# Two weight transfers in attention instead of three, early gathers split around a weight transfer, and smaller sink tiles

## The chip, the core and the metric

The kernel runs on one core of one Trainium2 chip. The metric is device microseconds for one execution. The time before is the median of 14 runs, 231.12 us. One further execution was taken with the hardware profiler, and all rows below are from it.

## The reference

Two layers follow one another. First, attention with 4 batches, 8 heads, 768 positions and head size 64. Three heads (0, 2 and 6) are causal over everything; the other five see the first 4 positions (the "sink") and a window of 64. Then a mixture of 8 experts over the 3072 tokens: a token's expert is given by `domain_id`, and no gate is computed.

```python
scores = scale * np.matmul(q, k.transpose(0, 1, 3, 2))
stream_keep = causal & (is_sink | in_win)       # heads that are not retrieval heads
a = softmax(np.where(mask, scores, -1e9))
x = np.matmul(a, v).transpose(0, 2, 1, 3).reshape(B * S, H * D)
for e in range(E):                              # 8 experts, D = 512, F = 1024
    mask = domain_id == e
    out[mask] = np.maximum(x[mask] @ w1[e], 0.0) @ w2[e]
```

## The kernel before

**Attention** is a loop over n = 0 to 16. Each n below 16 is a pair of heads of one batch: b = n // 4, and the pair is one of (0,2), (6,7), (1,3), (4,5). Iteration n computes the scores of pair n on PE (L302) and their exponentials on ACT (L339), transposes q and k of pair n+1 (PE L282, copied out by DVE L288), and multiplies the probabilities of pair n-1 with v (PE L391, "av", one PSUM tile for each of the two heads). DVE then divides by the row sums: a reciprocal (L403) and a multiply into the batch's tile `xb` (L404). Two PSUM buffers serve the transposes and the av tiles in turn, so an av tile waits for the multiply of the tile two before it. The last iteration, n = 16, has only the av of pair 15.

Ahead of each iteration `hooks(n)` queues the side work. SP loads q, k and v of pair n+4. POOL casts q and k of pair n+2 to 16 bits (L156), then v of pair n+1 (`cast_v`, L176, L180). `cast_v` also copies the 4 sink rows of v into the small tiles `vs`, which the av of streaming heads reads. When n is 5, 9 or 13, SP stores the finished batch `xb` to `x_tok` in DRAM (L415); the last batch is stored after the loop. POOL's queue also takes weight transfers (`load_w`, L187 for the first layer, L193 for the second; each reads 32-bit weights and writes 1 MB of 16-bit weights) and gathers (`load_xe`, L658), which fetch 128 tokens of an expert pair from `x_tok` by an index list. Every engine takes its own instructions in the order in which they stand.

**Routing** puts every token into a slot of its expert and makes the index lists on DVE, one item for each step of the loop; the last item is done in iteration 9.

**Experts** come in pairs pr = 0 to 3. A pair has seven gathers, g = 0 to 6. For pairs 0 and 1, g = 0, 1, 3 and 4 are the *early* gathers: they need only the tokens of batches 0 to 2 and are put into `hooks(14)`. Their tiles `xe` are cleared first by DVE (in `hooks(13)`). The early tokens go through the first layer (`layer1(e, 0, EARLY)`, PE L703, ACT L710) while the last batch is stored; then POOL gathers g = 2, 5 and 6, which need that store. Each gather is transposed on PE (`x_transpose`, L675) and copied out by DVE (L688, L682). The second layer (PE L754, L768) is copied out by DVE (L717) and scattered to `out` by POOL (L719).

The schedule is written by hand. What stands around the change:

```python
ws = {4: (0, 1), 8: (1, 1), 12: (2, 1)}
if n in ws:
    load_w(*ws[n])
...
if n == 14:
    for pr in range(2):
        for g in (0, 1, 3, 4):
            load_xe(pr, g, 3)
    load_w(3, 1)
```

After the loop the order is: `store_x(3)`; `x_transpose` of the early gathers of pair 0; `load_xe(0, 2/5/6)`; `load_w(0, 2)`; `load_xe(1, 2/5/6)`; `load_w(1, 2)`; four gathers of pair 2; `layer1` of expert 0's early tokens; `x_transpose` of pair 1's early gathers; `layer1` of experts 1, 2 and 3; then the transposes of g = 2, 5 and 6.

Of the kernel before, what the change touches and what calls it, by code (L numbers as in the profile page):

```python
# [9 lines left out]
FP16 = mybir.dt.float16  # L10
# [7 lines left out]
P = 128  # L18
# [3 lines left out]
def kernel(  # L22
# [14 lines left out]
    B, H, S, D = q.shape  # L37
    NTOK, DM = out.shape
    E, _, F = moe_w1.shape
    NS = int(n_sink)  # L40
# [13 lines left out]
    NSLOT = E * CAP  # L54
    PAIRS = [(0, 2), (6, 7), (1, 3), (4, 5)]
    NPAIR = B * len(PAIRS)
    scale = float(1.0 / np.sqrt(D))


# [49 lines left out]
    cpool = ctx.enter_context(tc.tile_pool(name="consts", bufs=1))  # L109
# [19 lines left out]
    out_i = cpool.tile([P, NSLOT // P], I32, name="out_i")  # L129
    flag_i = cpool.tile([1, 1], I32, name="flag_i")  # L130
    vs_t = [
        [cpool.tile([P, H, D + 1], FP16, name=f"vs{i}_{x}") for x in range(2)] for i in range(2)
    ]


    q32_t, qk_t, v_t, ve_t, w_t = {}, {}, {}, {}, {}
# [4 lines left out]
    def load_qk(n):  # L141
        b, pi = divmod(n, 4)
        hA, hB = PAIRS[pi]
        for nm, src in (("q", q), ("k", k)):
            t = qkpool.tile([P, 2, NSO, D], FP32, tag=nm, name=f"{nm}32_{n}")
            nc.sync.dma_start(
                out=t[:].rearrange("p h t d -> p h (t d)"),
                in_=hsel(src, b, hA, hB).rearrange("h (p t) d -> p h (t d)", p=P),
            )
            q32_t[nm, n] = t  # L150
# [19 lines left out]
    def cast_v(b, pi):  # L170
        if pi == 0:
            ve_t[b] = vepool.tile([P, NSO, H, D + 1], FP16, tag="ve", name=f"ve_{b}")
            nc.gpsimd.memset(ve_t[b][:, :, :, D : D + 1], 1.0)
        hA, hB = PAIRS[pi]
        for hh, h in enumerate((hA, hB)):
            nc.gpsimd.tensor_copy(out=ve_t[b][:, :, h, 0:D], in_=v_t[b, pi][:, hh])  # L176
        for hh, h in enumerate((hA, hB)):
            if not retr[h]:
                x = 1 if hh and not retr[hA] else 0
                nc.gpsimd.tensor_copy(  # L180
                    out=vs_t[b % 2][x][64 * x : 64 * x + NS, h, :], in_=ve_t[b][0:NS, 0, h, :]
                )

    def load_w(e, which):
        if which == 1:
            t = wpool.tile([P, 2, 2, F], FP16, tag="w1", name=f"w1_{e}")
            nc.gpsimd.dma_start(  # L187
                out=t[:].rearrange("p c r f -> p c (r f)"),
                in_=moe_w1[e].rearrange("(c p r) f -> p c (r f)", p=P, r=2),
            )  # L190
        else:
            t = wpool.tile([P, 2, 4, DM], FP16, tag="w2", name=f"w2_{e}")
            nc.gpsimd.dma_start(  # L193
                out=t[:].rearrange("p c r d -> p c (r d)"),
                in_=moe_w2[e].rearrange("(c p r) d -> p c (r d)", p=P, r=4),
            )
        w_t[e, which] = t
# [64 lines left out]
    def col_of(tiles, hh, jt, i):  # L262
        for n, (chunks, c0, c1) in enumerate(tiles):
            for c, h2, j2, i0, w in chunks:
                if (h2 == hh or (h2 == 2 and jt == "s")) and j2 == jt and i0 <= i < i0 + w:
                    return n, c + i - i0
        raise KeyError((hh, jt, i))
# [91 lines left out]
    def av_items(n):  # L359
        b, pi = divmod(n, 4)  # L360
        tiles = plans[pi]
        items = []
        for hh, h in enumerate(PAIRS[pi]):
            both_s = not any(retr[x] for x in PAIRS[pi])
            mms = []
            if retr[h]:
                for it in range(NSO):
                    for jt in range(it + 1):
                        mms.append((it, jt, 0, P))
            else:  # L370
                for it in range(NSO):
                    mms.append((it, it, 0, P))
                for it in range(2, NSO):
                    mms.append((it, "s", 0, P))
                mms.append((1, "s", 64, P))
                for it in range(1, NSO):
                    mms.append((it, it - 1, 0, 64))
            cell = {}

            def mm(x, h=h, hh=hh, mms=mms, cell=cell, both_s=both_s):  # L380
                it, jt, m0, m1 = mms[x]
                if x == 0:
                    cell["ps"] = ps_b.tile([P, 512], FP32, tag="b", name=f"av_{n}_{hh}")
                ps = cell["ps"][:, 0 : NSO * (D + 1)].rearrange("p (t d) -> p t d", t=NSO)
                r, c = col_of(tiles, hh, jt, it * P + m0)
                w = m1 - m0
                if jt == "s":
                    rhs = vs_t[b % 2][int(both_s and hh == 1)][:, h, :]
                else:
                    rhs = ve_t[b][:, jt, h, :]  # L390
                nc.tensor.matmul(  # L391
                    out=ps[m0:m1, it, :],
                    lhsT=eT[n, r // 3][:, r % 3, c : c + w],
                    rhs=rhs,
                    start=(x == 0),
                    stop=(x == len(mms) - 1),
                    skip_group_check=True,
                )
                if x == len(mms) - 1:
                    if b not in xb:  # L400
                        xb[b] = xpool.tile([P, NSO, DM], FP16, tag="xb", name=f"xb_{b}")
                    rcp = tpool.tile([P, NSO], FP32, tag="rcp", name=f"rcp_{n}_{hh}")
                    nc.vector.reciprocal(out=rcp[:], in_=ps[:, :, D])  # L403
                    nc.vector.tensor_tensor(  # L404
                        out=xb[b][:, :, h * D : (h + 1) * D],
                        in0=ps[:, :, 0:D],
                        in1=rcp[:].unsqueeze(2).to_broadcast([P, NSO, D]),
                        op=ALU.mult,
                    )

            items.append([lambda x=x, mm=mm: mm(x) for x in range(len(mms))])
        return items

# [233 lines left out]
    def xe_of(pr, g):  # L647
        u, o = (2 * pr + g // 3, g % 3) if g < 6 else ((pr, "h"), 0)
        if u not in xe_t:
            if g < 6:  # L650
                xe_t[u] = qkpool.tile([P, 3, DM], FP16, tag="qk"[u % 2], name=f"xe_{u}")
            else:
                xe_t[u] = vpool.tile([P, 1, DM], FP16, tag="v32", name=f"xeh_{pr}")
        return xe_t[u][:, o, :]

    def load_xe(pr, g, nb=B):
        s = pr * NG + g
        nc.gpsimd.indirect_dma_start(  # L658
            out=xe_of(pr, g),
            out_offset=None,  # L660
            in_=x_d[0 : 1 + nb * S, :],
            in_offset=bass.IndirectOffsetOnAxis(ap=map_i[:, s : s + 1], axis=0),
            bounds_check=nb * S,
            oob_is_err=False,
        )
# [135 lines left out]
    def hooks(n):  # L801
        b, pi = divmod(n, 4)
        if n + 4 < NPAIR:
            load_qk(n + 4)
            load_v((n + 4) // 4, (n + 4) % 4)
        if n + 2 < NPAIR:
            cast_qk(n + 2)
        if n + 1 < NPAIR:
            cast_v((n + 1) // 4, (n + 1) % 4)
        if n >= 5 and n % 4 == 1:  # L810
            store_x(n // 4 - 1)
        ws = {4: (0, 1), 8: (1, 1), 12: (2, 1)}
        if n in ws:
            load_w(*ws[n])
        if n == 13:
            for u in range(4):
                xe_of(u // 2, 3 * (u % 2))
                nc.vector.memset(xe_t[u][:, 0:2, :], 0.0)
        if n == 14:
            for pr in range(2):  # L820
                for g in (0, 1, 3, 4):
                    load_xe(pr, g, 3)
            load_w(3, 1)

    def run(fns):
# [5 lines left out]
    route = routing_items()  # L831
    for n in range(NPAIR + 1):
        if n < NPAIR:
            hooks(n)
        T = t_items(n + 1) if n + 1 < NPAIR else {"q": [], "k": []}
        A, B_ = av_items(n - 1) if n >= 1 else ([], [])
# [5 lines left out]
        else:  # L842
            h = len(B_) // 2
# [56 lines left out]
    with tc.If(nc.values_load(flag_i[0:1, 0:1], min_val=0, max_val=2) > 0, preferred_fallthrough_block=False):  # L900
        x_v = x_d[1 : 1 + NTOK, :].rearrange("(b p s) d -> b s p d", b=B, p=P)
        with tc.For_i(0, B, 1) as gb, tc.For_i(0, NSO, 1) as gs:
# [3 lines left out]
                out=g_d64[:], in_=moe_domain_id[bass.ds(t * P, P)].rearrange("(p c) -> p c", c=1)  # L906
# [6 lines left out]
            for c in range(4):  # L913
                c1, r = divmod(c, 2)
                nc.tensor.transpose(
                    out=gps[:, c, :],
                    in_=gx[:, c1 * 256 + r : (c1 + 1) * 256 : 2],
# [5 lines left out]
            for e in range(E):  # L923
# [15 lines left out]
                for f in range(8):  # L939
                    nc.tensor.matmul(  # L940
                        out=ps[:],
                        lhsT=hT_t[e][:, f, 0:P],
                        rhs=w_t[e, 2][:, f // 4, f % 4, :],
# [5 lines left out]
                    out=hit[:], in0=g_dom[:], scalar1=float(e), scalar2=None, op0=ALU.is_equal  # L949
                )  # L950
                if e == 0:
                    nc.vector.tensor_scalar(
                        out=acc[:], in0=ps[:], scalar1=hit[:], scalar2=None, op0=ALU.mult
                    )
                else:
                    nc.vector.scalar_tensor_tensor(
                        out=acc[:], in0=ps[:], scalar=hit[:], in1=acc[:],
# [38 lines left out]
```

## Time and profile before

| | |
|---|---|
| median of 14 runs | 231.12 us (228.88 to 232.08) |
| profiled execution, its own time | 228.71 us |
| its span, first to last instruction | 226.9 us |
| PE busy | 187.5 us (83%) |
| POOL busy | 117.2 us (52%) |
| DVE / ACT busy | 99.6 / 92.0 us |
| POOL's DMA queue (weights, gathers, scatters) | 26.75 MB, 51.7% of 16 DMA engines |
| SP's DMA queue (q, k, v, stores) | 22.62 MB, 34.8% |

PE, DVE, ACT, POOL and SP are the five engines; PEld is PE's weight load. A row of the timeline gives start, time, engine, line, operation, tiles, and in brackets the idle time of the engine ahead of it with what ended it ("remote": a semaphore for which the profile names no instruction). Attention ends at about 103 us of the span, the experts fill the rest.

### The profile page before, as it was taken

The numbers are of one execution on the slowest core, as the hardware profiler recorded it, in microseconds if no ns is written. First come the engines' busy times: TensorE is split into PE (matmuls) and PEld (weight loads), VectorE is DVE, ScalarE is ACT, GpSimd is POOL, SyncE is SP. The second block draws the span as 40 slices with busy tenths as digits, with TensorE's granted clock in tenths as the row PEclk, the third lists the DMA queues.
The fourth block names the chain that finished last, engine by engine and source line by source line (L and its number), as shares of the span: only waits on it lengthen the run. The fifth ranks groups of instructions, "written<-read, shape, count | busy, mean of one in ns | idle before, by whom it ended". The sixth has DMA issues, their size and how long they took to land. (4 is left out here: it accounts for less than half of the span.)

```text
span 226.9 us, 4808 instructions
## 1 busy us (share of the span) xinstructions
PE 187.5 (83%) x1959; PEld 122.5 (54%) x1959; DVE 99.6 (44%) x204; ACT 92.0 (41%) x120; POOL 117.2 (52%) x166
## 2 busy tenths in 40 slices
PE   1697878998699989629998699979999799999850
PEld 0365556666466556418997594446544455444330
DVE  1258999998857687214202102460024500343230
ACT  2575558766576784401565451005610055100000
POOL 4427679655627670770067754667536700017751
PEclk9999999999999999956999999999999999999995
DMA  7999999999999996239529999999799999904522
GB/s 203 314 300 274 282 315 295 224 350 331 258 269 339 322 189 180 72 109 151 182 52 174 194 258 246 276 239 255 206 214 241 240 275 215 185 4 155 213 84 94
DMA packets 42909, 49.79 MB, mean 219 GB/s; under 512 B 27263, under 2 KB 35712, under 8 KB 42882
## 3 DMA queue, kind: packets, MB, share of 16 engines
q0 software_dynamic: 7936, 26.75, 51.7%
q1 hardware_dynamic: 34802, 22.62, 34.8%
q8 instruction: 17, 0.28, 0.5%
q10 hardware_dynamic: 144, 0.07, 0.2%
q14 instruction: 10, 0.08, 0.1%
HBM read 56.76 MB, written 10.49 MB: 296 GB/s over the span
## 5 line engine op out<-in xcount | busy, mean ns | idle before, releaser
L339 ACT ACTIVATE eT<-sp 128x1024 f16<-128x1024 f32 (+2 forms) x68 | 57.3, 923 | 32.7 <-PE sp L302 30.6
L710 ACT ACTIVATE hT<-h 128x512 f16<-128x512 f32 (+2 forms) x48 | 32.1, 668 | 65.3 <-PE h L703 63.2
L703 PE MATMUL h<-xT,w 128*128 128x256 f16 (+2 forms) x384 | 50.2, 292 | 1.7 <-DVE xT L682 1.2
L719 POOL DMA_INDIRECT out_dram<-oute,out_i x27 | 27.0, 1000 | 41.3 <-DVE oute L717 38.2
L703 PEld LDWEIGHTS <-w 128*128 128x128 f16 x384 | 39.0, 114 | 12.1 <-DVE xT L682 1.1
L754 PE MATMUL o<-w,hT 128*128 128x512 f16 x184 | 41.1, 379 | 0.9 <-issue 0.9
L717 DVE COPY oute<-o 128x512 f32<-128x512 f32 x23 | 15.9, 691 | 56.9 <-PE o L754 51.7
L658 POOL DMA_INDIRECT xe<-x_tok,map_i x24 | 24.3, 1014 | 25.6 <-SPq L900 12.9
L391 PE MATMUL av<-ve,eT 128*128 128x65 f16 (+1 forms) x472 | 24.7, 197 | 7.8 <-DVE rcp L403 4.2
L754 PEld LDWEIGHTS <-hT 128*128 128x128 f16 x184 | 17.7, 98 | 23.1 <-issue 2.8
L391 PEld LDWEIGHTS <-eT 128*128 128x128 f16 (+1 forms) x572 | 22.1, 102 | 13.8 <-DVE rcp L403 4.3
L302 PE MATMUL sp<-qT,kT 64*128 64x192 f16 (+8 forms) x276 | 23.9, 276 | 4.5 <-DVE kT L288 4.5
L156 POOL CAST q<-q 128x768 f16<-128x768 f32 x15 | 12.9, 862 | 21.2 <-DMA q<-in_q_dram 13.1
L302 PE MATMUL sp<-c16s 128*128 128x128 f16 (+1 forms) x132 | 22.4, 272 | 1.3 <-ACT eT L339 0.8
L302 PEld LDWEIGHTS <-kT 64*128 64x128 f16 (+1 forms) x276 | 10.8, 96 | 14.5 <-DVE kT L288 7.1
L404 DVE TENSOR_TENSOR xb<-av,rcp 128x384 f16<-128x384 f32 x32 | 17.8, 557 | 1.1
L688 DVE COPY xT<-xtp 128x1024 f16<-128x1024 f16 (+1 forms) x16 | 8.2, 552 | 22.5 <-PE xtp L675 22.5
L176 POOL CAST ve<-v 128x384 f16<-128x384 f32 x32 | 15.7, 518 | 4.0 <-DMA v<-in_v_dram 3.8
L288 DVE COPY qT<-tpq 128x768 f16<-128x768 f16 x15 | 14.2, 950 | 6.0 <-PE tpq L282 5.7
L288 DVE COPY kT<-tpk 128x768 f16<-128x768 f16 x16 | 15.2, 950 | 3.6 <-PE tpk L282 3.6
L156 POOL CAST k<-k 128x768 f16<-128x768 f32 x15 | 12.9, 857 | 7.3 <-PE av L391 3.3
L302 PEld LDWEIGHTS <-c16s 128*128 128x128 f16 x132 | 9.9, 101 | 6.0 <-issue 3.3
(83 smaller groups left out, 136.2 us busy)
## 6 DMA issues: line engine op xcount, KB each, us to landing
w<-in_moe_w_dram POOLq DMA_DIRECT2D x16, 1024.0 KB
q<-in_q_dram SPq DMA_DIRECT2D x16, 384.0 KB, 6.3
k<-in_k_dram SPq DMA_DIRECT2D x16, 384.0 KB, 6.1
v<-in_v_dram SPq DMA_DIRECT2D x32, 192.0 KB, 6.0
x_tok<-xb SPq DMA_DIRECT2D x4, 768.0 KB, 7.4
out_dram<-oute,out_i POOLq DMA_INDIRECT x27
xe<-x_tok,map_i POOLq DMA_INDIRECT x24
c16s<-c SPq DMA_DIRECT2D x1, 336.5 KB, 6.0
```

The lines of the kernel that those rows point to most:

```text
L156: eng.tensor_copy(out=t[:].rearrange("p t h d -> p h t d"), in_=q32_t[nm, n][:])
L288: evac(out=d[:], in_=cell["ps"][:, 0:NSO].rearrange("d t p -> d p t"))
L302: nc.tensor.matmul(out=sp[rows, c : c + w], lhsT=lhsT, rhs=rhs, start=bank not in begun, stop=True, skip_group_check=True,)
L339: nc.scalar.activation(out=eT[n, r // 3][:, r % 3, c0:c1], in_=sp[:, c0:c1], func=AF.Exp, scale=scale)
L391: nc.tensor.matmul(out=ps[m0:m1, it, :], lhsT=eT[n, r // 3][:, r % 3, c : c + w], rhs=rhs, start=(x == 0), stop=(x == len(mms) - 1), skip_ ...
L404: nc.vector.tensor_tensor(out=xb[b][:, :, h * D : (h + 1) * D], in0=ps[:, :, 0:D], in1=rcp[:].unsqueeze(2).to_broadcast([P, NSO, D]), op=A ...
L658: nc.gpsimd.indirect_dma_start(out=xe_of(pr, g), out_offset=None, in_=x_d[0 : 1 + nb * S, :], in_offset=bass.IndirectOffsetOnAxis(ap=map_i ...
L703: nc.tensor.matmul(out=pv[:, a, c0:c1], lhsT=w_t[e, 1][:, c // 2, c % 2, fc * 512 + fr : (fc + 1) * 512 : 4], rhs=xT_t[e][:, c, c0:c1], st ...
L710: nc.scalar.activation(out=hT_t[e][:, 2 * f2 : 2 * f2 + 2, c0:c1], in_=pv[:, :, c0:c1], func=AF.Relu)
L717: nc.vector.tensor_copy(out=o[:], in_=ps[:])
L719: inst = nc.gpsimd.indirect_dma_start(out=out, out_offset=bass.IndirectOffsetOnAxis(ap=out_i[:, s : s + 1], axis=0), in_=o[:], in_offset=None,
L754: nc.tensor.matmul(out=ps[:], lhsT=hT_t[e][:, f, g * P : (g + 1) * P], rhs=w_t[e, 2][:, f // 4, f % 4, :], start=(f == 0), stop=(f == 7),)
```

## The change

The first-layer weights of experts 0 and 1 move from hooks 4 and 8 to hooks 6 and 12; those of expert 2 leave the loop's middle and go to hook 14. The early gathers of pair 0 go from hook 14 to hook 13 and so stand ahead of `cast_v(3, 3)` on POOL; those of pair 1 stay in hook 14, now between the weights of experts 2 and 3. The clearing of the `xe` tiles goes from hook 13 to hook 12. The `vs` tiles keep only the heads that they serve.

```diff
+    VS = [[7, 1, 4], [3, 5]]
...
-        [cpool.tile([P, H, D + 1], FP16, name=f"vs{i}_{x}") for x in range(2)] for i in range(2)
+        [cpool.tile([P, len(VS[x]), D + 1], FP16, name=f"vs{i}_{x}") for x in range(2)]
+        for i in range(2)
...
-                    out=vs_t[b % 2][x][64 * x : 64 * x + NS, h, :], in_=ve_t[b][0:NS, 0, h, :]
+                    out=vs_t[b % 2][x][64 * x : 64 * x + NS, VS[x].index(h), :],
+                    in_=ve_t[b][0:NS, 0, h, :],
...
-                    rhs = vs_t[b % 2][int(both_s and hh == 1)][:, h, :]
+                    x_ = int(both_s and hh == 1)
+                    rhs = vs_t[b % 2][x_][:, VS[x_].index(h), :]
...
-        ws = {4: (0, 1), 8: (1, 1), 12: (2, 1)}
+        ws = {6: (0, 1), 12: (1, 1)}
         if n in ws:
             load_w(*ws[n])
-        if n == 13:
+        if n == 12:
             for u in range(4):
                 xe_of(u // 2, 3 * (u % 2))
                 nc.vector.memset(xe_t[u][:, 0:2, :], 0.0)
+        if n == 13:
+            for g in (0, 1, 3, 4):
+                load_xe(0, g, 3)
         if n == 14:
-            for pr in range(2):
-                for g in (0, 1, 3, 4):
-                    load_xe(pr, g, 3)
+            load_w(2, 1)
+            for g in (0, 1, 3, 4):
+                load_xe(1, g, 3)
             load_w(3, 1)
```

In the built programs the instructions of PE, ACT and SP stand in the same order before and after; one weight load of PE (the first of expert 2) gets a wait for the transfer of its weights.

## Prediction

> **What bounds the kernel now.** I read the page's slices first, then the PE waits, then the timelines of PE, POOL and DVE around 80 to 131 us, where the change acts.
>
> ```profile
> PE   1697878998699989629998699979999799999850
> PEclk9999999999999999956999999999999999999995
> DMA  7999999999999996239529999999799999904522
> ```
>
> A slice is 5.67 us. PE is nearly full in attention and in the experts, and has one hole, the slices from 90.8 to 102.1 us; there the DMA engines are slack too, and the granted clock falls. In attention the DMA engines are full until about 79 us, but PE does not pay for it: between 6 and 95 us PE's weight loads wait for POOL's casts, which wait for inputs, 1.2 us in all. From 131 us to the end PE waits little. So the time is set by how fast attention ends and how soon PE runs again.
>
> ```profile
> 91.91 0.36 PE L391 MATMUL av<-ve,eT 128*128 128x65 f16 x6
> 93.26 0.36 PE L391 MATMUL av<-ve,eT 128*128 128x65 f16 x6
> 95.18 0.34 PE L391 MATMUL av<-ve,eT 128*128 128x65 f16 x6 [1.16 <-DVE xb L404]
> 96.53 0.59 PE L391 MATMUL av<-vs,eT 128*128 128x65 f16 x5 [1.01 <-ACT eT L339]
> 101.56 0.52 PE L391 MATMUL av<-ve,eT 128*128 128x65 f16 x6 [4.22 <-DVE rcp L403]
> 103.20 1.87 PE L675 MATMUL xtp<-c16s,xe 128*128 128x128 f16 x16 [0.48 <-DVE rcp L403]
> ```
>
> ```profile
> 94.24 0.20 DVE L403 RECIPROCAL rcp<-av 128x6 f32<-128x6 f32 x1 [2.96 <-PE av L391]
> 100.72 0.20 DVE L403 RECIPROCAL rcp<-av 128x6 f32<-128x6 f32 x1 [5.69 <-remote]
> 102.26 0.20 DVE L403 RECIPROCAL rcp<-av 128x6 f32<-128x6 f32 x1 [0.76 <-remote]
> ```
>
> ```profile
> 84.14 0.52 POOL L180 COPY vs<-ve 4x65 f16<-4x65 f16 x2
> 90.73 1.09 POOL L658 DMA_INDIRECT xe<-x_tok,map_i  x1 [6.07 <-DVE rcp L403]
> 99.99 1.00 POOL L658 DMA_INDIRECT xe<-x_tok,map_i  x1 [0.30 <-issue]
> 100.98 0.78 POOL L187 DMA_DIRECT2D w<-in_moe_w_dram  x1
> 114.62 1.05 POOL L658 DMA_INDIRECT xe<-x_tok,map_i  x1 [12.86 <-SPq L900]
> ```
>
> The second head of pair 14 is through PE at 94.02 (its last rows begin 93.68 and take 0.34), yet DVE takes it up only at 100.72, with nothing to do since 95.03. The first head of pair 14 ends at 92.66 and is taken up at 94.24. PE's completions reach DVE late while the eight early gathers run (90.73 to 100.99). A weaker case stands at 127.73 to 129.76, where DVE takes up transposes that PE ended at 128.46, beside POOL's gather of 128.07. Between 80 and 88 us, beside a weight transfer and no gather, I see no such lag. So I read it as a cost of gathers moving data, not of weight transfers; the trace does not prove that.
>
> ```profile
> 121.34 0.40 PE L675 MATMUL xtp<-c16s,xeh 128*128 128x128 f16 x4 [0.46 <-DMA xeh<-x_tok,map_i]
> 130.24 0.39 PE L675 MATMUL xtp<-c16s,xeh 128*128 128x128 f16 x4 [1.77 <-DVE xT L688]
> ```
>
> After 103.20 PE is dense up to these two waits, which hang on gathers behind the last store. PE has 0.46 + 1.77 = 2.2 us of waiting there: the end follows the store of the last batch (issued 103.77, its gathers from 114.62), and PE's own start only beyond that.
>
> **The change part by part.** *Transfers out of hooks 4 and 8, one into hook 6.* The 26.75 MB of POOL's queue took 51.7% of 226.9 us = 117.3 us, so a 1.05 MB transfer is 4.6 us of all engines. PE gets at most the 1.2 us above; the casts' input waits are covered because POOL runs two pairs ahead. Taken 0, bounds -1.2 and +1 (if the one in hook 6 delays pair 10).
>
> *Smaller vs tiles.* Four memsets, 1.93 us at 0.75, shrink to about a third; POOL then waits 3.81 us for v anyway. 0. The matmuls keep 65 columns.
>
> *Memsets one hook sooner.* The four take 2.11 us on DVE (81.32 to 83.43) and now stand ahead of the first reciprocal of iteration 12 instead of 13. There PE waited 0.46 us at 84.13 for the late multiply; the same stall moves to 77 or so and may delay the store of batch 2. 0, bounds -0.5 and +0.8.
>
> *Pair 0's gathers ahead of `cast_v(3,3)`.* The first gather waits for the store of batch 2, issued after 81.3, so POOL still starts it at 90.73 (w of expert 1 now lies beside that store where expert 2's did; POOL waited 2.18 us for q ahead of it, so up to 2.2 sooner; 0.8 later through the memsets). Behind the waiting gather stand, new, the two casts and two sink copies of pair 15, done at 84.66 before. Now: four gathers to 96.0 (starts 1.3 us apart), then 1.43 us as at 83.23 to 84.66, so 97.4. Who waits is PE: pair 15's av began at 95.18. Its first head ends at about 98.0 (0.81 us for the rows from 96.53, after the first sink copy at 97.1) and its second at 99.1 (1.16 us as at 101.56). From PE's end to the store took 103.77 - 102.72 = 1.05 us: store at 100.2, 3.6 us sooner, if completions are on time. They should be, because the first four gathers are over by 97 and a weight transfer, not gathers, moves data next; for late completions I take 1.0 us, bounds 0 and 5.0 (the lag from 95.7 to 100.7). Store at 101.2: -2.6 us.
>
> *Weights of expert 2 ahead of pair 1's gathers, then expert 3's.* POOL issues them at 97.5, the gathers from 98.5 to 103.7, expert 3's at about 104 (100.98 before). Transfer 4.6 us and some 1.5 us of lead: expert 2 lands at about 104, the gathers at 106 to 107, expert 3 at about 112. PE wants pair 1 at 105 to 108 (108.90 before), expert 2 after 111, expert 3 after 114: at most 1.5 us of wait, inside the 2.2 us of slack. The store, though, lies beside two transfers instead of one. The trace has four stores, 5.9 to 10.1 us to landing; the last took 10.1 and POOL woke 0.75 later. Bounds 5.9 and 10.1 + 4.6; taken 10.6, so that -2.6 becomes -2.1 at the late gathers and at the end.
>
> A rule weighed on PE's side: in this trace the clock is 0.50 in 101 to 104 us and full again by the slice from 107.7. The Trainium skill (TensorE: Matmul & The Clock Gate, What's actually happening) says that one busy window of about 3.4 us gives the full clock back. By it PE, busy from 97.1, would have it some 3 us sooner and keep the whole 4 us of its earlier start. By the row alone (6 matmuls of the first layer in 1.24 us at half clock, 207 ns each, 32 of them 6.6 us against 4.07) PE keeps 1.5 us, which with its 2.2 us of slack is still over 2.1.
>
> **Sum.** 228.71 - 2.1 = 226.6 for an execution like the profiled one. That one was 2.41 us under the median of the runs shown; the same distance gives 229.0 us.
>
> **Rivals.** *Slower: the completions stay late through the second burst.* If PE's results of pair 15 reach DVE only when the second four gathers and expert 3's issue are over (about 104.2), the store goes out at 105.2, 1.4 later than before, with both transfers still to share engines: landing costs up to 2.5 more. +1.4 to +3.9, about 233.6. It decides from the point where the store is later than 103.77. For it: lags of 1.6 to 6.7 us in the trace, and the hold of `cast_v` itself, which without any lag before would cost 97.4 - 95.2 = 2.2 us. Against it: the transfer between the bursts.
>
> *No change.* The store goes out 2.6 us sooner and lands 2.6 us later, at 12.7 us. Against it: 10.1 was with a whole transfer beside it. 231.1.
>
> *Inputs count after all.* The transfers out of the middle give 1.2 us, POOL reaches hook 13 2.2 us sooner, and the store is out at 99: -4.3, about 226.8. Against it: PE's waits in attention are for DVE copies, not for inputs.
>
> **How the numbers follow.** About 0.3% (0.7 us) is what a measurement of this kernel can tell from no change. Forecast (0.7 to 3.5 us faster) 0.42, inputs count 0.08, no change 0.12, slower 0.38. So faster 0.50, same 0.12, slower 0.38. The range goes from 226.8 to 233.8, which leaves out the far end of the slower rival, where both the lag and the sharing are at their bounds. The forecast's own range is 227.6 to 230.4.
>
> **What would show it.** Right: gathers of pair 0 at about 90.7 and then the casts of pair 15 behind them on POOL, av of pair 15 from about 97, the DVE idle of 5.69 us gone, the last store at 100 to 102, the first late gather at 111 to 113, the wait at 130.24 earlier by some 2 us. Wrong: a reciprocal of pair 15 at 103 or later, a last store after 103.8, a first late gather after 114.6, or PE waiting over 2 us for pair 1's gathers or expert 3's weights.

## Result, and the profile after

The changed kernel takes 227.64 us (median of 10 runs, 226.63 to 231.03), the kernel before beside it 230.68 us (median of 47). The ratio is 0.9879, 95% interval 0.9851 to 0.9908: 1.2% faster. The prediction was 229.0 us (226.8 to 233.8), with 0.50 on faster.

Some executions of either kernel take over 1.5% more than its fastest; medians and ranges are of all runs, ratios and their intervals leave these out, and the profile taken with the result caught one (231.55 us). So the rows of after are from a further profiled execution of the same kernel, 226.53 us with a span of 224.7 us (run e6 below). Against the profiled execution of before this is 2.2 us less. Lines above 56 have moved: L403 is now L407, L658 is L662, L675 is L679.

The slices first, 5.62 us each: PE, its granted clock, the DMA engines.

```profile
PE   0797979997989889696997899979999799999740
PEclk9999999999999999959999999999999999999985
DMA  7999999999999991399799998999899999614512
```

The hole of a 6 and a 2 is now a 6, a 9 and a 6. The timelines of PE (end of attention), DVE and POOL show why, and SP's with the last store, first before and then after:

```profile
94.85 0.40 PE L395 MATMUL av<-ve,eT 128*128 128x65 f16 x4 [0.66 <-ACT eT L342]
97.34 1.04 PE L679 MATMUL xtp<-c16s,xe 128*128 128x128 f16 x8
98.86 1.01 PE L679 MATMUL xtp<-c16s,xe 128*128 128x128 f16 x8 [0.49 <-DVE xb L408]
106.62 0.40 PE L679 MATMUL xtp<-c16s,xe 128*128 128x128 f16 x4 [1.72 <-DMA xe<-x_tok,map_i]
118.24 0.38 PE L679 MATMUL xtp<-c16s,xeh 128*128 128x128 f16 x4 [0.29 <-DVE xT L692]
126.20 0.38 PE L679 MATMUL xtp<-c16s,xeh 128*128 128x128 f16 x4 [0.29 <-issue]
```

```profile
91.29 0.20 DVE L407 RECIPROCAL rcp<-av 128x6 f32<-128x6 f32 x1 [1.32 <-PE sp L305]
93.03 0.20 DVE L407 RECIPROCAL rcp<-av 128x6 f32<-128x6 f32 x1 [0.96 <-remote]
96.36 0.20 DVE L407 RECIPROCAL rcp<-av 128x6 f32<-128x6 f32 x1 [1.56 <-PE av L395]
97.93 0.20 DVE L407 RECIPROCAL rcp<-av 128x6 f32<-128x6 f32 x1 [0.78 <-PE av L395]
```

```profile
86.91 1.09 POOL L662 DMA_INDIRECT xe<-x_tok,map_i  x1 [5.90 <-DVE xb L408]
92.00 0.96 POOL L178 CAST ve<-v 128x384 f16<-128x384 f32 x2
93.37 0.75 POOL L190 DMA_DIRECT2D w<-in_moe_w_dram  x1
99.40 0.78 POOL L190 DMA_DIRECT2D w<-in_moe_w_dram  x1
107.52 1.05 POOL L662 DMA_INDIRECT xe<-x_tok,map_i  x1 [7.34 <-SPq L907]
```

```profile
103.77 0.36 SPq L415 DMA_DIRECT2D x_tok<-xb  x1
98.74 0.36 SPq L419 DMA_DIRECT2D x_tok<-xb  x1
```

DVE's longest wait for an av result is 1.56 us, where it was 5.69. The first gather goes out at 86.91 (90.73 before), PE begins the transposes of pair 0 at 97.34 (103.20), the last store is issued at 98.74 on SP (103.77), the first late gather starts at 107.52 (114.62), and the waits of 0.46 and 1.77 us ahead of the late transposes are down to 0.29 each. New is PE's 1.72 us for the gathers of pair 1, behind the weights of expert 2.

One measure carries what follows: the time from the reciprocal of pair 12's second head to that of pair 15's second head, the last one of attention. It is 86.39 to 102.97 = 16.6 us in the profile of before, and 85.24 to 97.93 = 12.7 us here. With nothing late it is 9.4 us (e12, and e1, e3, e4, e8 and e10 below).

### The profile page after: what moved, and what is told of

Its sections match the earlier page's. It is cut to its first block, busy times and chain, and to the rows that moved or that the text cites. A ratio compares the mean times of both kernels' runs of the same rounds, so it can differ in the third digit from the quotient of the medians.

```text
span 229.8 us, 4809 instructions
## 1 busy us (share of the span) xinstructions
PE 190.6 (83%) x1959; PEld 123.8 (54%) x1959; DVE 100.4 (44%) x204; ACT 92.1 (40%) x120; POOL 115.8 (50%) x166
## 5 line engine op out<-in xcount | busy, mean ns | idle before, releaser
L707 PE MATMUL h<-xT,w 128*128 128x256 f16 (+2 forms) x384 | 52.0, 299 | 1.7 <-DVE xT L686 1.2
L707 PEld LDWEIGHTS <-w 128*128 128x128 f16 x384 | 40.2, 116 | 12.7 <-DVE xT L686 1.2
L662 POOL DMA_INDIRECT xe<-x_tok,map_i x24 | 24.4, 1018 | 23.3 <-SPq L907 11.3
L305 PE MATMUL sp<-qT,kT 64*128 64x192 f16 (+8 forms) x276 | 24.7, 282 | 5.9 <-DVE kT L291 5.8
L158 POOL CAST q<-q 128x768 f16<-128x768 f32 x15 | 12.4, 824 | 23.1 <-PE tpq L285 10.5
L178 POOL CAST ve<-v 128x384 f16<-128x384 f32 x32 | 16.2, 531 | 6.5 <-DMA v<-in_v_dram 6.4
L305 PEld LDWEIGHTS <-c16s 128*128 128x128 f16 x132 | 10.1, 103 | 5.8 <-issue 3.4
```

The lines of the kernel that those rows point to most:

```text
L158: eng.tensor_copy(out=t[:].rearrange("p t h d -> p h t d"), in_=q32_t[nm, n][:])
L305: nc.tensor.matmul(out=sp[rows, c : c + w], lhsT=lhsT, rhs=rhs, start=bank not in begun, stop=True, skip_group_check=True,)
L662: nc.gpsimd.indirect_dma_start(out=xe_of(pr, g), out_offset=None, in_=x_d[0 : 1 + nb * S, :], in_offset=bass.IndirectOffsetOnAxis(ap=map_i ...
L707: nc.tensor.matmul(out=pv[:, a, c0:c1], lhsT=w_t[e, 1][:, c // 2, c % 2, fc * 512 + fr : (fc + 1) * 512 : 4], rhs=xT_t[e][:, c, c0:c1], st ...
```

## Experiments

They were run in three sets, each beside the kernel before on its own chip. That kernel took 219.61 us on the chip of the first set, 231.73 on that of the second and 219.80 on that of the third; the result's chip (230.68) is like the second's. This difference is itself the main finding. Medians are compared only within a set; where rows of two sets stand side by side, the text says so.

**First set (before: 219.61 us, median of 17).**

*e1: the changed kernel, for its profile on the chip of the set.*

> The changed kernel itself, for a profile to set beside the one before. Theory A (the last batch's store goes out sooner, because a weight transfer instead of four gathers follows the first burst): 2 to 3.5 us under the kernel before, last store issued at 100 to 102 us (103.77 before), first late gather at 111 to 113 (114.62). Theory B (fewer weight transfers beside the input loads shorten attention itself): the same gain, but the scores of pair 12 already begin a us or more sooner than 74.8.

224.14 us, ratio 1.0185 (1.0137 to 1.0233): here the change makes the kernel 1.9% slower, against both theories; the gains expected of its parts (e2, e3) do not come either. In the timelines of PE and POOL:

```profile
94.33 1.30 PE L679 MATMUL xtp<-c16s,xe 128*128 128x128 f16 x16 [0.28 <-DVE rcp L407]
104.99 1.89 PE L679 MATMUL xtp<-c16s,xe 128*128 128x128 f16 x16 [5.62 <-DMA xe<-x_tok,map_i]
```

```profile
92.62 0.75 POOL L190 DMA_DIRECT2D w<-in_moe_w_dram  x1
97.65 1.00 POOL L662 DMA_INDIRECT xe<-x_tok,map_i  x1 [0.30 <-issue]
105.54 1.05 POOL L662 DMA_INDIRECT xe<-x_tok,map_i  x1 [6.11 <-SPq L907]
```

No result of PE is late on this chip (9.4 us from pair 12 to pair 15), so PE is through attention at 94.33 and stands 5.62 us before pair 1's gathers, which were issued by 98.7 but lie behind the 1 MB of expert 2. The Trainium skill (DMA: Bandwidth & Descriptors, Two DMAs through the same engine are not ordered) says that the descriptors within one queue of one DMA engine start in order; this wait agrees.

*e2: only the gathers and the clearing are moved, the weights stay.*

```diff
-        if n == 13:
+        if n == 12:
             for u in range(4):
...
+        if n == 13:
+            for g in (0, 1, 3, 4):
+                load_xe(0, g, 3)
         if n == 14:
-            for pr in range(2):
-                for g in (0, 1, 3, 4):
-                    load_xe(pr, g, 3)
+            for g in (0, 1, 3, 4):
+                load_xe(1, g, 3)
             load_w(3, 1)
```

> The kernel before with one part of the change: pair 0's early gathers in hook 13 and the clearing in hook 12; weights stay in hooks 4, 8 and 12, pair 1's gathers stay in hook 14. Theory A: only 1.4 us of casts lie between the two bursts, so PE's completions of pair 15 stay late beside the second one; 0 to -1.5 us. Theory B: no gain (0), since the weights stay. If the move of the gathers is the whole of it: -2.8 us as in the change.

221.29 us, ratio 1.0062 (1.0024 to 1.0100). PE's timeline:

```profile
97.00 0.49 PE L391 MATMUL av<-ve,eT 128*128 128x65 f16 x6 [2.24 <-POOL ve L176]
```

Here pair 15's casts are held behind four waiting gathers and PE pays 2.24 us: the first gather starts at 91.37. In e1 it starts at 86.15, the casts are done at 92.7, and PE has no such wait.

*e3: only the weights are moved; all gathers stay in hook 14.*

```diff
-        ws = {4: (0, 1), 8: (1, 1), 12: (2, 1)}
+        ws = {6: (0, 1), 12: (1, 1)}
...
         if n == 14:
-            for pr in range(2):
-                for g in (0, 1, 3, 4):
-                    load_xe(pr, g, 3)
+            for g in (0, 1, 3, 4):
+                load_xe(0, g, 3)
+            load_w(2, 1)
+            for g in (0, 1, 3, 4):
+                load_xe(1, g, 3)
             load_w(3, 1)
```

> The kernel before with the other part: weights in hooks 6, 12 and 14, those of expert 2 between the gathers of pair 0 and pair 1, all gathers still in hook 14 behind the casts. Theory A: the transfer splits the burst and nothing holds the casts, so -1.5 to -3.5 us. Theory B: the whole gain, -2.8. If the gathers' earlier hook is what counts: 0.

223.22 us, ratio 1.0175 (1.0129 to 1.0220): the whole loss of e1. PE waits 1.25 + 0.63 + 1.54 + 0.49 = 3.9 us for the four gathers of pair 1. The first gather of pair 0 starts at 87.50, against 91.37 in e2: it is the weights' place, not the gathers', that makes it early.

*e4: the changed kernel with the casts of pair 15 ahead of pair 0's gathers.*

```diff
-        if n + 1 < NPAIR:
+        if n + 1 < NPAIR and n != 14:
             cast_v((n + 1) // 4, (n + 1) % 4)
+        if n == 13:
+            cast_v(3, 3)
```

> The changed kernel with the casts and sink copies of pair 15 put ahead of pair 0's gathers in hook 13. Theory A with the hold as I priced it: pair 15's av can start at 95 instead of 97, the store goes out up to 2 us sooner, 0.5 to 1.5 us under the changed kernel. If late completions set pair 15 and not the hold: 0 against the changed kernel, within 0.7 us.

224.29 us, ratio 1.0178 (1.0128 to 1.0227), as e1; PE waits 6.15 us for pair 1. The pair of runs isn't clean, since the first gather too comes later here (88.86 against 86.15). But with no wait for the casts in e1 and no gain from moving them, the hold, a term of my sum, costs the changed kernel nothing that shows on this chip.

**Second set (before: 231.73 us, median of 19).**

*e5: the kernel before, unchanged, for its profile.*

> The kernel before, for its profile on the chip of these runs. The first four experiments ran on a chip where the kernel before takes 219.6 us and where no profile shows a late completion of PE. If late completions (as in the profile before) belong to the chip: on a chip at 219 to 221 us the reciprocals of pair 14 follow PE within 0.3 us and the last store is issued at 96 to 99 us; on a chip at 229 to 232 us the lags of 1.5 to 6.7 us are there and the store is issued near 103.8.

233.44 us, ratio 0.9943 (0.9879 to 1.0006). DVE's timeline, of an execution of 233.03 us, which serves only to confirm the first profile:

```profile
95.16 0.20 DVE L403 RECIPROCAL rcp<-av 128x6 f32<-128x6 f32 x1 [2.88 <-PE av L391]
103.10 0.20 DVE L403 RECIPROCAL rcp<-av 128x6 f32<-128x6 f32 x1 [7.15 <-remote]
```

From pair 12 to pair 15 it is 17.7 us. The eight gathers stand from 91.53 to 101.77 on POOL; the result that PE ended near 95 is taken up at 103.10.

*e6: the changed kernel.*

> The changed kernel once more. If the sign of the change hangs on the late completions: 1.5 to 2.2% slower than the kernel before on a chip without them (PE waits 4 to 6 us for pair 1's early gathers behind the weights of expert 2), 0.7 to 1.5% faster on a chip with them (the last store 2 us or more sooner). If it hangs on something else of the chip, the sign does not go with the lags.

229.15 us, ratio 0.9859 (0.9763 to 0.9954), so this chip repeats the result. Its profile is the one shown above, the fastest of its four runs.

*e7: the changed kernel with pair 1's gathers ahead of both weight transfers, so that only the casts (1.4 us) part the bursts.*

```diff
         if n == 14:
-            load_w(2, 1)
             for g in (0, 1, 3, 4):
                 load_xe(1, g, 3)
+            load_w(2, 1)
             load_w(3, 1)
```

> The changed kernel with hook 14 in another order: pair 1's gathers first, then the weights of expert 2, then of expert 3. Without late completions: PE's wait for pair 1's gathers (5.6 us) goes, 3 to 4.5 us under the changed kernel, at most 0.5% over the kernel before (the casts of pair 15 are still held). If the wait moves to expert 2's weights: 0 to 1.5 us. With late completions: the second burst directly follows the casts, so pair 15 completes late, 0.5 to 2 us over the changed kernel.

230.24 us, ratio 0.998 (0.993 to 1.003): most of the gain is gone (the interval overlaps the end of that of e6 and lies clear of the result's). DVE's timeline and POOL's, of an execution of 232.35 us, 2.1 us above the median:

```profile
98.53 0.20 DVE L407 RECIPROCAL rcp<-av 128x6 f32<-128x6 f32 x1 [2.20 <-PE av L395]
100.80 0.20 DVE L407 RECIPROCAL rcp<-av 128x6 f32<-128x6 f32 x1 [1.48 <-PE xtp L679]
```

```profile
112.54 1.06 POOL L662 DMA_INDIRECT xe<-x_tok,map_i  x1 [11.18 <-SPq L907]
```

Pair 12 to pair 15 takes 14.4 us against 12.7 in e6, and the store, now right behind both transfers, is seen landed at 112.54 instead of 107.52. Of these 5.0 us, 1.2 stand there before pair 12 and 1.7 arise between the pairs; 2.1 are the landing itself, 10.6 us after the issue instead of 8.4. PE does not wait for pair 1's gathers. By the two ratios, e7 is 1.2% slower than e6 (of which the ratio has two runs). So the place of the transfer earns more on this chip than the 1.72 us that it costs, but how much of that is lateness and how much is the store's landing is not shown.

*e8: the kernel before with the clearing and all eight early gathers behind the loop.*

```diff
-        if n == 13:
-            for u in range(4):
-                xe_of(u // 2, 3 * (u % 2))
-                nc.vector.memset(xe_t[u][:, 0:2, :], 0.0)
         if n == 14:
-            for pr in range(2):
-                for g in (0, 1, 3, 4):
-                    load_xe(pr, g, 3)
             load_w(3, 1)
...
     store_x(B - 1)
+    for u in range(4):
+        xe_of(u // 2, 3 * (u % 2))
+        nc.vector.memset(xe_t[u][:, 0:2, :], 0.0)
+    for pr in range(2):
+        for g in (0, 1, 3, 4):
+            load_xe(pr, g, 3)
```

> The kernel before with the clearing of the xe tiles and all eight early gathers behind the loop, so that no gather runs before the last av; the weights of expert 3 stay in hook 14. A test of what delays PE's completions: with gathers as the cause, pair 14 and pair 15 are taken up by DVE within 0.3 us of their last matmul on every chip and the last store is issued by 99.5 us; if the lag stays without gathers, its cause is another one. The first gathers then stand on PE's path, so the whole is 3 us or more over the kernel before on a chip without lags.

238.17 us, ratio 1.0247 (1.0158 to 1.0335). DVE at the end of attention, then ACT and PE in the first expert layer:

```profile
93.33 0.20 DVE L403 RECIPROCAL rcp<-av 128x6 f32<-128x6 f32 x1 [0.57 <-PE av L391]
94.38 0.20 DVE L403 RECIPROCAL rcp<-av 128x6 f32<-128x6 f32 x1 [0.26 <-PE av L391]
```

```profile
113.78 0.60 ACT L710 ACTIVATE hT<-h 128x512 f16<-128x512 f32 x1 [2.28 <-remote]
118.30 0.60 ACT L710 ACTIVATE hT<-h 128x512 f16<-128x512 f32 x1 [3.92 <-remote]
```

```profile
113.80 0.28 PE L703 MATMUL h<-xT,w 128*128 128x256 f16 x1 [0.47 <-issue]
118.94 3.57 PE L703 MATMUL h<-xT,w 128*128 128x256 f16 x16 [3.02 <-ACT hT L710]
123.25 6.28 PE L703 MATMUL h<-xT,w 128*128 128x256 f16 x56 [0.74 <-ACT hT L710]
```

With no gather in attention, the same chip delivers every av result at once (9.4 us from pair 12 to pair 15), and the lateness has moved with the gathers (96.68 to 121.63 on POOL): ACT takes up the last of expert 0's four results at 113.78, though PE was through with that expert at 108.49. This shows that on this chip the early gathers make PE's results late. The kernel is slower all the same, and by the same lateness: PE waits 5.16 us for pair 0, yet starts its transposes at 100.19, sooner than in the two profiles of before on late chips (103.20 and 105.03); but the 96 matmuls of experts 1 to 3, 10.64 us there, last from 109.23 to 129.53.

**Third set (before: 219.80 us, median of 13).** It was meant to part gathers from weights on a chip where results are late, and to try a better version. Its chip turned out to be one where none is late.

*e12: the kernel before, for its profile.*

> The kernel before once more, for its profile on the chip of these runs. If the chip takes about 230 us for it, DVE waits 4 us or more for a result of pair 14 or 15 that PE had long ended (5.69 us in the first profile). If the chip takes about 220 us, no such wait is over 1.5 us, the last store is issued at about 97 us or sooner, and the rows at 121 and 130 us of the first profile have no wait beyond 2 us.

218.58 us, span 216.8 us. DVE and PE:

```profile
92.04 0.20 DVE L403 RECIPROCAL rcp<-av 128x6 f32<-128x6 f32 x1 [1.42 <-PE av L391]
93.39 0.20 DVE L403 RECIPROCAL rcp<-av 128x6 f32<-128x6 f32 x1 [0.57 <-PE av L391]
94.44 0.20 DVE L403 RECIPROCAL rcp<-av 128x6 f32<-128x6 f32 x1 [0.26 <-PE av L391]
```

```profile
95.38 1.07 PE L675 MATMUL xtp<-c16s,xe 128*128 128x128 f16 x12 [0.28 <-DVE rcp L403]
102.36 1.06 PE L675 MATMUL xtp<-c16s,xe 128*128 128x128 f16 x12 [1.32 <-DMA xe<-x_tok,map_i]
```

It is the same program as in the first profile, with gathers at the same place (from 90.01), but the wait of 5.69 us is one of 0.57, and PE starts pair 0's transposes at 95.38 instead of 103.20. Next to e1 (of the first set, whose kernel before is 0.19 us faster) it shows the loss there: pair 0 starts 1.05 us sooner with the change, pair 1's transposes 2.6 us later (104.99 against 102.36). Then comes the clock. Windows of PE in e12, then in e1 (window, length, busy, granted clock, DMA share, GB/s):

```profile
104.00:106.00 2.00, 2.00 (x21) 1.00 1.03 207
106.00:108.00 2.00, 2.00 (x21) 1.00 1.05 252
```

```profile
104.00:106.00 2.00, 1.01 (x10) 0.50 1.10 241
106.00:108.00 2.00, 2.00 (x16) 0.50 1.06 215
```

PE's pause in e1 has cost it the full clock, and the 96 first-layer matmuls of experts 1 to 3 take 12.06 us instead of 10.64. The spans differ by 221.0 - 216.8 = 4.2 us.

*e9 and e10: the kernels of e2 and e3 again.*

> The kernel before with the gathers of pair 0 moved to hook 13, ahead of the casts of pair 15, and the clearing one hook sooner; the weights stay where they were (hooks 4, 8 and 12, expert 3 behind the gathers of pair 1). Two theories on the gain of the whole change. Theory G: the gain is that the two bursts of gathers no longer lie whole over the end of attention, so that PE's results reach DVE sooner; then, on a chip where results are late beside gathers, this part alone brings most of the gain: 0.6 to 1.2% faster than before, last store 2 us or more sooner. Theory T: the gain needs a weight transfer between the bursts, since only there is the queue free of gathers; then this part alone, with only the casts (1.4 us) between the bursts, is within 0.4% of before and DVE still waits 4 us or more for a result of pair 14 or 15. On a chip where no result is late, both expect 0.6% slower (the hold of the casts, about 1.4 us), as in the earlier run of this edit.

> The kernel before with its weights as in the change (hooks 6 and 12, expert 2 in hook 14 between the gathers of pair 0 and pair 1, expert 3 behind), with all gathers in hook 14 behind the casts of pair 15. Theory G: the place of the first burst matters, so this part alone is at most half of the gain (0 to 0.6% faster) on a chip where results are late beside gathers. Theory T: the transfer between the bursts is the gain: 0.8 to 1.5% faster, since the casts are also not held. On a chip where no result is late, both expect 1.7% slower (PE waits some 4 us for the gathers of pair 1 behind the transfer), as in the earlier run of this edit.

221.57 us, ratio 1.0066 (1.0022 to 1.0109), and 222.96 us, 1.0137 (1.0074 to 1.0201), as each theory expected of a chip where nothing is late. Between the two theories the set decides nothing. The hold of e9 is 1.48 + 0.30 us at PE; e10 waits 3.25 + 0.40 + 0.43 us for pair 1.

*e11: meant to beat both kernels. e2 with the weights of expert 3 ahead of pair 1's gathers.*

```diff
         if n == 14:
+            load_w(3, 1)
             for g in (0, 1, 3, 4):
                 load_xe(1, g, 3)
-            load_w(3, 1)
```

> A version meant to beat both: the gathers of pair 0 in hook 13 as in the change, but the weights of experts 0, 1 and 2 in hooks 4, 8 and 12 as before, and in hook 14 the weights of expert 3 ahead of the gathers of pair 1, so that a transfer parts the bursts and only one transfer lies beside the last store. On a chip where results are late beside gathers: Theory T expects it 0.3 to 1.0 us faster than the changed kernel, that is 1.3 to 1.7% faster than before, with the last store's data visible 1 to 2 us sooner than in the changed kernel. Theory G expects it like the gathers alone, 0.6 to 1.2% faster. On a chip where no result is late: 1.5 to 2% slower than before, since the gathers of pair 1 still stand behind 1 MB in the queue and PE waits for them some 4 to 5.6 us, as in the changed kernel.

228.01 us, ratio 1.0301 (1.0216 to 1.0386), worse than the 1.5 to 2% expected. PE, then POOL:

```profile
97.81 0.34 PE L391 MATMUL av<-ve,eT 128*128 128x65 f16 x6 [2.46 <-POOL ve L176]
110.54 1.89 PE L675 MATMUL xtp<-c16s,xe 128*128 128x128 f16 x16 [4.43 <-DMA xe<-x_tok,map_i]
```

```profile
111.42 0.99 POOL L658 DMA_INDIRECT xe<-x_tok,map_i  x1 [6.79 <-SPq L902]
```

It has both costs, the hold of e2 and the wait of e3, and the second begins only where the first has ended. I had counted one. On a chip with late results it was not run.

## Why the prediction came out right, step by step

**What bound the kernel: right.** The end of attention held the store, and DVE's wait was for results that PE had long ended. "A cost of gathers moving data, not of weight transfers" was argued from one trace; e8 shows the first half of it: take the gathers away and the lateness is gone, put them elsewhere and it is there. e7 against e6 is what the second half expects, by one comparison in which the store's landing changes too. What I could not see in one trace is that the lateness is there in some sets of runs only.

**First gather at 90.73, "up to 2.2 sooner": mis-sized.** It came at 86.91. From the issue of the store of batch 2 to this gather it takes 5.8 to 6.5 us in six executions with the weights of the change (e1, e3, e6, e7, e10 and the profile with the result), and 9.0 to 10.0 us in six with those of before (both profiles of before, e2, e9, e11, e12). e3 and e2 show that it is the weights' move, not the gathers'. What divides the groups in these runs is how old hook 12's transfer is when the store is issued: 5.4 to 5.8 us in the first, 2.7 to 4.3 in the second. e4 fits: it has the weights of the change, but a transfer only 4.6 us old, and takes 9.2. With a transfer less in the loop, POOL issues hook 12's transfer at 74.89 in e6 instead of 78.30. I had taken the part as nothing for PE, and looked past the store.

**The hold, 1.43 us at 97.4: not on the path.** The casts ended at 93.4. The rival's price for the hold "without any lag before", 2.2 us, is what e2 paid (2.24), where the gate was not early.

**Late completions, 1.0 us (0 to 5.0): too small, in range.** Above the 9.4 us of a prompt chip, before loses 7.2 us and e6 still loses 3.3: 2.0 at pair 13 beside the first burst, the rest beside the second. The slower rival's mechanism is real at that size, and did not decide, since results came while the second burst was still going out.

**Store at 101.2: too late; landing of 10.6 us: too long.** The store is issued 5.0 us sooner than before, not 2.6, and POOL sees it landed 8.4 us after the end of its issue, where it was 10.5; I had added 0.5 us for the second transfer. In all runs in which POOL waits for this landing there are two groups: 8.4 to 11.0 us where a weight transfer was issued up to 6 us ahead of the store (ten executions, both profiles of before among them), 4.5 and 4.6 us where one came only behind (e2, e9). In e12, where POOL did not wait, it is at most 5.1. So on a chip without lateness the store of the kernel before escapes ahead of expert 3's weights (96.30 against 100.28); on a late chip it slips behind them (104.13 against 100.98) and pays about 5 us more. In every run of the changed kernel a transfer goes out ahead of the store, and the landing takes 8.4 us or more.

**-2.1 us at the end: right in sum, not in its parts.** -7.1 us at the late gathers did not reach the end. Against the profile of before, PE gains 5.9 us at pair 0, 2.9 at the first layer of expert 1 (109.79 to 106.86), 4.0 at the last late transposes, 3.7 at the first `o2h` (141.59 to 137.93), 2.2 at the end. The first drop is the step that failed: "at most 1.5 us of wait, inside the 2.2 us of slack" ignored that PE, once early, stands there itself. Of the 2.9 us, 1.72 are that wait, 0.5 the clock (4.57 us for expert 0's matmuls against 4.07), and the rest goes in the transposes of the two pairs. The last 1.5 us are lost around the final scatters, where results are late as well. So it is luck that 2.2 us at the end is so near the 2.1 of the sum: the gate, the store and the landing were each better than I had them, by 5.0 us at the late gathers, and losses that I had not counted took that away again.

The clock in e6 is 0.50 from 95.0 to 101.5 us and 1.00 after. PE was busy from 95.50 but for 0.49 us just ahead of 98.86, so the full clock came 6.0 us after the first of these and 2.7 after the second. Where PE worked without a gap, it came 4.6 us after the start in e1 (104.99 to about 109.6) and 5.6 in e4 (105.75 to about 111.3). The Trainium skill (TensorE: Matmul & The Clock Gate, What's actually happening) has the full clock back after about 3.4 us of sustained work; the measured delay is longer in e1 and e4, and not a fixed one. As the rule had it, the clock came back sooner than before (there at about 105.9).

One execution of each, on chips that may differ, is no proof of each step; the medians fell by 3.0 us here and by 2.6 in the second set.

**Rivals.** "Inputs count after all", given 0.08, had the right early gate and a store at 99, and put the whole gain at the end, twice what the profiles show. "Slower" holds in the first set, by what I had listed only as a sign of being wrong: PE waiting over 2 us for pair 1's gathers (5.62 in e1). The third set ran only parts of the change; e10, with its weights, is 1.4% slower.

**Open.** Why two chips deliver PE's results promptly beside gathers and others do not. Each of the three chips was seen in one set of runs only, so it isn't shown either that the chip decides, and not something else at that time. Whether PE's matmuls finish late or only word of them is late: the profile models the ends of matmuls, and in the late stretches PE itself stops between single matmuls, for 0.2 to 0.5 us and without a wait that the profile names (e8 from 110.19, e6 at 92.01 and 92.73; none in e1 and e12 from 86 to 94 us). The share of gathers and of weights in the gain, since those parts ran only where there is no gain. The smaller `vs` tiles and the earlier clearing did not run alone; e3, which has neither, loses what e1 does (1.75% and 1.85%). Whether attention itself became shorter is open too: the reciprocal of pair 12's second head, ahead of all this, stands anywhere from 84.45 to 88.64 us in the fourteen executions.

## What to carry to other kernels

Before shortening a wait, ask on which chips it exists: the same edit was worth -1.2% where PE's results were late beside gathers and +1.9% where they were not. A transfer put between two bursts of gathers paid off only in the set with late results; its price is that the gathers behind it land one transfer later, and that PE, once ahead, stops there and drops its clock (5.62 us and 0.50 in e1). A store on the path should go out ahead of a megabyte of weights, not behind it: it landed after 4.5 and 4.6 us or after 8.4 to 11.0 us in these runs.

## What the runs showed of the hardware that was not expected

The same program takes 219.6 and 219.8 us on two chips and about 231 us in the other runs. The difference that the profiles show is how soon PE's results arrive beside indirect DMAs (gathers and scatters): up to 8 us late (e5, from 95.0 to 103.10). Of the 10.1 us between the spans of the first profile and of e12, 7.2 arise from pair 12 to pair 15. The scatters at the very end show it too: DVE takes up the last `o2h` at 210.91 in e6, where PE ended it at 208.59, and at 204.31 in e12, where PE ended it at 204.24; and PE's last matmuls wait longer for the copies. First e6, then e12:

```profile
210.91 0.69 DVE L721 COPY oute<-o2h 128x512 f32<-128x512 f32 x1 [3.44 <-PE o L758]
217.04 1.38 PE L742 MATMUL o_last<-w,hT 128*128 128x256 f16 x8 [2.62 <-ACT oute_last L750]
```

```profile
204.31 0.69 DVE L717 COPY oute<-o2h 128x512 f32<-128x512 f32 x1 [1.19 <-PE o2h L768]
209.36 1.03 PE L738 MATMUL o_last<-w,hT 128*128 128x256 f16 x8 [0.68 <-ACT oute_last L746]
```

In e12 the clock of 88 to 118 us is 1.00 in every window: the half clock that I had read as part of the kernel came with PE's pauses behind the late results.
